# Values products regrouped from five bursts a pair to three, with their outputs copied out one unit later (attention and gated FFN, one core)

## The chip, the cores and the metric

The kernel runs on one core of one Trainium2 chip. The metric is the device time of one execution in microseconds (us), as the median of several runs. TensorE (PE) multiplies and transposes, VectorE (DVE), ScalarE (ACT) and GpSimd (POOL) work on elements, SyncE (SP) issues transfers.

## The reference, cut to what matters

```python
# q, k, v: (4, 8, 576, 64); the bias comes from a small network over the distance of two positions
scores = q @ k.transpose(0, 1, 3, 2) / 8 + bias[None]
attn = softmax(scores, axis=-1)
x = (attn @ v)                                  # the values products, (4, 8, 576, 64)
x = x.transpose(0, 2, 1, 3).reshape(4, 576, 512)
h = relu(x @ w_in)                              # 512 -> 1024
conv = depthwise_conv3(h, conv_w)               # along the sequence
out = (h * sigmoid(conv)) @ w_out               # (4, 576, 512), float32
```

## The kernel before, in words

The span has three parts. In the first 66 us the position bias is computed, written to memory, and the first attention work starts. Until about 285 us the attention runs. After that comes the feed-forward part. The change touches only the attention.

The attention goes through 16 pairs: a pair `n` is two heads of one batch. A pair has five units `t` = 0 to 4 (also called by `ui`, the same number): unit 0 holds the 64 left-over rows of both heads, units 1 to 4 hold 128 rows of each head. The list `flat` gives the units in order, and in the loop's turn for unit u each engine gets, in this order:

- PE: the scores of unit u+2 (`scores`, L349; one score tile for each head, a single one when u+2 is a unit 0). A score tile takes two PSUM banks, and the pool `psS` holds two such tiles. So the first scores of a unit can start only when the first reduction of the unit before has read its tile, and the second scores when the second reduction, and the small copy behind it, have read theirs. Then the `side` transposes (L408; none in unit 0, and L412 for the sums in unit 2), which write into the second score tile; then the transposes of unit u's probabilities (`transposes`, L420, into two of the three `psT` banks); then some parts of the values products (`pv_parts`, L457).
- DVE: the reductions of the scores of unit u+2 (`reduce`, L360: bias added, result to SBUF, row minimum kept), then the copies of unit u's transposed probabilities into `ptx` or `pty` (L91), a step of a weight-splitting job (L97 or L103), and in unit 0 the inversion of the sums (L472, L473).
- ACT: the exponentials of unit u+1 (`expo`, L374), the other copy of unit u's transposed probabilities (L88), a job step (L99), and, where a values group has ended, its copy from PSUM to `x` (L88, `act(xb...)`).

The values products of a pair come in two groups: group 0 (320 columns, from `ptx`) is complete after unit 2, group 1 (256 columns, from `pty`) after unit 4 of the pair. Each group has five parts, a part being two products (one for each head). The parts wait in the deque `fill`, and `pv_share[ui]` says how many are issued at the end of a unit. The single bank of `psO` holds a group's sum, so one group must be copied out before the next begins. In the trace each product shows as two matmul records: one part is four records, a 128-row unit's scores are eight.

Of the kernel before, what the change touches and what calls it, by code (L numbers as in the profile page):

```python
# [9 lines left out]
F32 = mybir.dt.float32  # L10
# [9 lines left out]
def attention_ffn_kernel(  # L20
# [12 lines left out]
    B, S, DM = out.shape  # L33
    NP = qk.shape[1]
# [4 lines left out]
    P = 128  # L39
# [30 lines left out]
    x_p = pool(ctx, "x", B)  # L70
# [16 lines left out]
    def act(o, i):  # L87
        nc.scalar.activation(o, i, AF.Copy)  # L88
# [45 lines left out]
    with tc.manual_schedule():  # L134
# [56 lines left out]
        x0 = x_p.tile([P, NP, S], F32, name="x0", tag="x")  # L191
# [77 lines left out]
        def bias_out(blk):  # L269
            nf, nr = reach(blk)  # L270
            n = max(nf, nr + 1)
            ps = bias_ps.pop(blk)
            st = sts[blk // 2 % 5].rearrange("p (b n) -> p b n", b=2)
            if n > 512:
                o, i = st[:, blk % 2:blk % 2 + 1], ps.rearrange("p (b a) x -> p b (a x)", b=1)
            else:
                o, i = st, ps
            fwd = nf > nr


            if n > 512 or blk % 2:
                k = relu_from(blk) - 3
                for oo, ii in (
                    (slice(nr, nr + nf), slice(0, nf)) if fwd else (slice(0, nr + 1), slice(nr, None, -1)),
                    (slice(0, nr), slice(nr, 0, -1)) if fwd else (slice(nr + 1, nr + nf), slice(1, nf)),
                ):
                    nc.scalar.activation(o[:, :, oo], i[:, :, ii], AF.Identity, bias=kv[:, k:k + 1], scale=inv_scale)  # L287
            if blk % 2 == 0:
                return
            at = 64 + (blk - 1) * P * BW - nr  # L290
            dst = bias_d[at:at + 2 * P * BW].rearrange("(b p c) -> p b c", b=2, c=BW)
            nc.sync.dma_start(dst[:, :, 0:nr + nf], st[:, :, 0:nr + nf])
# [33 lines left out]
        def turned_sp(n, t):  # L326
            tile = sp_p.tile([P, 2 * S + 2], F32R, name="sr", tag=spt[n, t][1])
            nc.scalar.activation(tile[:, 2 * S:], pars[:, 0:2], AF.Copy)
            spt[n, t] = (tile, None)
# [107 lines left out]

        ops_t = {}
        waiting = {}

        def pv_parts(n, g):
            p, b = seq[n]

            waiting[n] = waiting.get(n, 0) + 1
            x0, width = (XW, YW) if g else (0, XW)

            def part(c):
                pt, vt = ptt[n, g], vts[n]
                if c == 0:
                    ops_t[n, g] = psO.tile([P, 512], F32, name="o")  # L450
                po = ops_t[n, g]
                for h in range(2):
                    if c == 4:
                        slot, blk = (9 if h else 4), 4
                    else:
                        slot = blk = 5 + c if h else c
                    nc.tensor.matmul(  # L457
                        po[D * h:D * h + D, 0:width], vt[:, slot, :], pt[:, blk, :],
                        start=(c == 0), stop=(c == 4),
                    )  # L460
                if c == 4:
                    del ptt[n, g]
                    waiting[n] -= 1
                    if b not in xb:
                        xb[b] = x_p.tile([P, NP, S], F32, name=f"x{b}", tag="x")
                    act(xb[b][:, p, x0:x0 + width], po[:, 0:width])

            return [lambda c=c: part(c) for c in range(5)]

        def invert(n):  # L470
            sm, r = sms.pop(n), rr_t[n % 2][:, 0:9]
            nc.vector.tensor_scalar(r, sm, 1e-9, None, op0=ALU.add)  # L472
            nc.vector.reciprocal(r, r)  # L473
# [120 lines left out]
        for i in range(NBLK):  # L594
            nxt = bias_hidden(i + 1) if i + 1 < NBLK else None
            bias_mm(i, hidden)
            if last:
                bias_out(*last)
            last = (i,)
            hidden = nxt  # L600
            if i % 8 == 6 % 8 and i >= 6:
                load_bias(0, (i - 6) // 8)
            if i == 1:
                load_v(0)
            if i == 16:
                load(1)
            if i == 20:
                load_v(1)
            if i % 8 == 13 % 8 and i >= 13:
                unit = unit_steps(*first[(i - 13) // 8])  # L610
            if unit:
                next(unit, None)
            if fill:
                fill.popleft()()
        bias_out(*last)
        load_bias(0, 4)
        while fill:
            fill.popleft()()
        for _ in unit:
            pass  # L620
        for u in range(2):
            for h in heads(flat[u][1]):
                reduce(scores(*flat[u], h), *flat[u], h)
            if u == 0:
                for h in heads(flat[0][1]):
                    expo(*flat[0], h)
                turned_sp(*flat[0])
        pv_share = (2, 2, 1, 3, 2)
        hs_ff = {}
        raw_w = {}  # L630
        job_steps = iter(())
# [3 lines left out]
        for u, (n, t) in enumerate(flat):  # L635
            p, b = seq[n]
            ui = units.index(t)
            sums = n - 1 if ui == 2 and n else None
            side = None
            if u + 2 < NU:  # L640
                for h in heads(flat[u + 2][1]):
                    if side is not None:
                        reduce(side, *flat[u + 2], 0)
                    side = scores(*flat[u + 2], h)
            if t:
                if side is None:
                    side = psS.tile([P, 2, 512], F32, name="s")
                side_transposes(side, n, t, sums)
            if u + 2 < NU:
                reduce(side, *flat[u + 2], h)  # L650
            if u + 1 < NU:
                for h in heads(flat[u + 1][1]):
                    expo(*flat[u + 1], h)
                turned_sp(*flat[u + 1])
            transposes(n, t, side, sums)
            next(job_steps, None)

            parts = len(fill) if u < 5 else pv_share[ui]
            while fill and parts > 0:
                fill.popleft()()  # L660
                parts -= 1
            next(job_steps, None)
            del spt[n, t]
            if u + 2 >= NU:
                f = u + 2 - NU
                hs_ff[0, f] = ffn_in(0, f)
            if u == 1 or n and ui == 2 and n + 2 < NSEQ:
                load(2 if u == 1 else n + 2)
            if u in conv_weights:
                conv_weights[u]()  # L670

            for at, do in ((u - 7, "load"), (u - 11, "split")):
                job = at // 2
                if at % 2 == 0 or not 0 <= job < 4 * KC + 2 * FE:
                    continue
                if job < 4 * KC:
                    src, dst = w_in[job // 4 * P:job // 4 * P + P], wi[job // 4]
                else:
                    src, dst = w_out[(job - 4 * KC) // 2 * P:(job - 4 * KC) // 2 * P + P], wo[(job - 4 * KC) // 2]
                cs = slice(job % 4 * 256, job % 4 * 256 + 256) if job < 4 * KC else slice(job % 2 * 256, job % 2 * 256 + 256)  # L680
                if do == "load":
                    raw_w[job] = (e_p if job % 3 else woe_p).tile([P, 256, 2], I32, name="raw_w", tag="h")
                    load_w(raw_w[job], src[:, cs])
                else:
                    job_steps = split_w_steps(e_p, dst[:, :, cs], raw_w.pop(job), ("cv", "cv"))
            if u + 2 < NU:
                n2, t2 = flat[u + 2]
                p2, b2 = seq[n2]
                if b2 == B - 1 and p2 + 1 < NP:
                    load_bias(p2 + 1, t2)  # L690
            if ui == (0 if n > 1 else 1) and n > 0:
                invert(n - 1)
            if ui == (2 if n > 1 else 3) and 1 <= n and n + 1 < NSEQ:
                load_v(n + 1)
            if ui == 3 and n > 0:
                store_sums(n - 1)
            if ui == 4 and n > 0:
                spread_sums(n - 1)
            if ends_group(n, t):
                fill.extend(pv_parts(n, t > 2))  # L700

            if ui == 2 and n > 1:
                apply_norm(n - 2)
            if n == NSEQ - 2 and ui > 1:
                x_parts(0, ui - 2)
            if n == NSEQ - 1 and ui == 0:
                x_parts(0, 3)
            if n == NSEQ - 1 and ui in (1, 2):
                load_wo(FE - 1 + ui)
        while fill:  # L710
            fill.popleft()()
        invert(NSEQ - 1)
        turn_sums(NSEQ - 1)
        apply_norm(NSEQ - 2)
# [200 lines left out]
```

## Time and profile before

| | us |
|---|---|
| median of 3 runs | 504.41 |
| the runs | 501.97, 504.41, 504.76 |
| the profiled execution, whole time | 501.91 |
| its span, first to last instruction | 500.1 |
| PE busy | 479.1 (96%) |
| DVE busy | 386.5 (77%) |
| ACT busy | 311.1 (62%) |
| POOL busy | 103.4 (21%) |
| PE's share of the chain that ended last | 87% |
| values products (L457) in that chain | 18% |

The span is 1.81 us shorter than the profiled execution's own time. A busy PE is read with care, since matmuls overlap and their ends are modelled; what an operation costs on PE is therefore read from the start of one group of records to the start of the next, not from the busy time of a group.

### The profile page before, as it was taken

The numbers are of one execution on the slowest core, as the hardware profiler recorded it, in microseconds if no ns is written. First come the engines' busy times: TensorE is split into PE (matmuls) and PEld (weight loads), VectorE is DVE, ScalarE is ACT, GpSimd is POOL, SyncE is SP. The second block draws the span as 40 slices with busy tenths as digits, with TensorE's granted clock in tenths as the row PEclk, the third lists the DMA queues.
The fourth block names the chain that finished last, engine by engine and source line by source line (L and its number), as shares of the span: only waits on it lengthen the run. The fifth ranks groups of instructions, "written<-read, shape, count | busy, mean of one in ns | idle before, by whom it ended". The sixth has DMA issues, their size and how long they took to land.

```text
span 500.1 us, 11125 instructions
## 1 busy us (share of the span) xinstructions
PE 479.1 (96%) x4202; PEld 352.5 (70%) x4202; DVE 386.5 (77%) x875; ACT 311.1 (62%) x747; POOL 103.4 (21%) x121
## 2 busy tenths in 40 slices
PE   5988899999999999999999999899999999999994
PEld 3333256666666666666666689779988999899884
DVE  6999957888899988889898729974994299649900
ACT  5888877878888889888887736622632154126400
POOL 1000000103232313323336215620080005200000
PEclk9999999999999999999999999999999999999999
DMA  5779556488778977788751300002000200020011
GB/s 138 268 248 333 213 176 150 109 234 225 171 167 211 250 177 177 200 221 260 189 147 56 113 16 26 1 1 85 0 1 8 92 8 1 1 85 1 2 63 42
DMA packets 32703, 60.83 MB, mean 122 GB/s; under 512 B 5490, under 2 KB 12170, under 8 KB 32650
## 3 DMA queue, kind: packets, MB, share of 16 engines
q1 hardware_dynamic: 32506, 60.04, 42.2%
q8 instruction: 33, 0.54, 0.5%
q14 instruction: 20, 0.16, 0.1%
q10 hardware_dynamic: 144, 0.08, 0.1%
HBM read 44.12 MB, written 15.98 MB: 120 GB/s over the span
## 4 chain that ended last, share of the span: by engine, by line
PE 87%; DVE 5%; ACT 5%; issue 1%; DMA 1%; DVEq 0%; ACTq 0%
PE o L457 18%; PE s L518 17%; PE s L349 16%; PE tp L766 15%; PE tp L420 9%; PE s L261 6%; PE o L766 4%; ACT st L287 2%; DVE cv L741 2%; PE s L408 1%; DVE sp L360 1%; ACT y L240 1%; DMA pars<-in_par_dram 1%; ACT sp L374 1%; DVE cv L748 1%
## 5 line engine op out<-in xcount | busy, mean ns | idle before, releaser
L360 DVE CUSTOM_DVE_ANT_0 sp<-s,bt 128x576 f32<-128x576 f32 x144 | 104.2, 754 | 32.0 <-PE s L349 14.5
L374 ACT ACTIVATE sp<-sp,nm 128x576 f32<-128x576 f32 x144 | 109.9, 767 | 1.4 <-DVE nm L360 1.4
L518 PE MATMUL s<-xs,wi 128*128 128x288 f32 x768 | 103.8, 296 | 1.7 <-ACT h L530 1.7
L518 PEld LDWEIGHTS s<-xs,wi 128*128 128x128 f32 x768 | 102.8, 189 | 3.2 <-ACT h L530 2.0
L349 PE MATMUL s<-qk 64*128 64x288 f32 (+1 forms) x640 | 93.1, 431 | 1.8 <-DVE nm L360 1.1
L349 PEld LDWEIGHTS s<-qk 64*128 64x128 f32 (+1 forms) x640 | 46.8, 175 | 44.8 <-DVE nm L360 13.0
L766 PE MATMUL tp<-wo,g 128*128 128x512 f32 x288 | 70.5, 390 | 0.0
L420 PE MATMUL tp<-identr,sr 64*128 64x64 f32 x1184 | 64.3, 247 | 0.0
L741 DVE SCALAR_TENSOR_TENSOR cv<-h,cw,cv 128x575 f32<-128x575 f32 x64 | 60.6, 946 | 2.5 <-ACT cv L736 0.6
L766 PEld LDWEIGHTS tp<-wo,g 128*128 128x128 f32 x288 | 53.7, 188 | 11.6 <-DVE g L761 0.7
L420 PEld LDWEIGHTS tp<-identr,sr 64*128 64x128 f32 x1184 | 55.5, 136 | 5.7 <-issue 0.6
L457 PE MATMUL o<-ptx,vt 128*64 128x320 f32 x320 | 50.4, 443 | 1.3 <-ACT ptx L88 0.9
L261 PE MATMUL s<-y,pars 128*32 128x512 f32 (+8 forms) x352 | 46.5, 504 | 5.0 <-ACT st L287 2.2
L530 ACT ACTIVATE h<-s 128x576 f32<-128x576 f32 x32 | 20.8, 650 | 47.7 <-PE s L518 47.7
L497 POOL TENSOR_TENSOR x<-x,rb 128x576 f32<-128x576 f32 x16 | 23.6, 1473 | 128.6 <-ACT sp L374 94.2
L244 DVE TENSOR_SCALAR y<-tl,inv,nb 128x512 f32<-128x512 f32 (+8 forms) x116 | 49.9, 506 | 0.1
L457 PE MATMUL o<-pty,vt 128*64 128x256 f32 x320 | 44.2, 393 | 0.0
L261 PEld LDWEIGHTS s<-y,pars 128*32 128x32 f32 x352 | 16.4, 113 | 32.8 <-DVE y L244 17.4
L747 ACT ACTIVATE cv<-cv 128x576 f32<-128x576 f32 x32 | 21.8, 683 | 28.4 <-DVE cv L741 28.4
L91 DVE COPY ptx<-tp 128x256 f32<-128x256 f32 (+1 forms) x64 | 32.0, 500 | 1.4 <-PE tp L420 1.2
L131 POOL TENSOR_SCALAR xs<-x 128x576 fp32r<-128x576 f32 x16 | 14.8, 924 | 81.5 <-PE s L518 81.5
L88 ACT ACTIVATE ptx<-tp 128x256 f32<-128x256 f32 (+1 forms) x64 | 26.4, 438 | 7.9 <-PE tp L420 7.3
(75 smaller groups left out, 570.6 us busy)
## 6 DMA issues: line engine op xcount, KB each, us to landing
qk<-in_qk_dram SPq DMA_DIRECT2D x32, 320.0 KB
bt<-bias_d SPq DMA_DIRECT2D x32, 288.0 KB
bias_d<-st SPq DMA_DIRECT2D x14, 607.0 KB
qk<-in_qk_dram SPq DMA_DIRECT2D x32, 144.0 KB
rb<-r_d SPq DMA_DIRECT2D x32, 144.0 KB
out_dram<-o SPq DMA_DIRECT2D x17, 256.0 KB
raw_w<-in_moe_w_in_dram SPq DMA_DIRECT2D x16, 256.0 KB
raw_w<-in_moe_w_out_dram SPq DMA_DIRECT2D x12, 256.0 KB
```

The source lines that it names most:

```text
L88: nc.scalar.activation(o, i, AF.Copy)
L91: nc.vector.tensor_copy(o, i)
L244: nc.vector.tensor_scalar(y, dist[:, 0:n], inv[:, ig:ig + 1], nb1, op0=ALU.mult, op1=ALU.max)
L261: nc.tensor.matmul(ps[32 * j:32 * j + 32, a // 512 if n > 512 else blk % 2, 0:min(n - a, 512)], w2b, ys[j][:, a:min(n, a + 512)], start=Tr ...
L349: nc.tensor.matmul(ps[po, a, 0:HS], qt[rows, qo:qo + po.stop - po.start], qt[rows, KO + hh * HS:KO + hh * HS + HS], start=True, stop=True,)
L360: nc.vector.tensor_tensor_reduce(out=halves(spt[n, t][0][:, h]), in0=ps[:, :, 0:HS], in1=halves(bt[:, h]), op0=ALU.add, op1=ALU.min, scale ...
L374: exps[n, t, h] = nc.scalar.activation(sp[:, h], sp[:, h], AF.Exp, bias=nm[:, h:h + 1], scale=-1.0, accum_out=sms[n][:, col:col + 1],)
L420: tr = nc.tensor.transpose(ps[a][:, TL * s:TL * s + TL].bitcast(F32R), spf[ra, j:j + P], identr[ra, ra])
L457: nc.tensor.matmul(po[D * h:D * h + D, 0:width], vt[:, slot, :], pt[:, blk, :], start=(c == 0), stop=(c == 4),)
L518: nc.tensor.matmul(ps[:, a, 0:HS], wi[c][:, pw, cs], xss[b, c][:, px, a * HS:(a + 1) * HS], start=(i == 0), stop=(i == 3 * KC - 1),)
L741: nc.vector.scalar_tensor_tensor(out=cv[:, o:o + S - 1], in0=h[:, i:i + S - 1], scalar=cw[:, f, kk:kk + 1], in1=cv[:, o:o + S - 1], op0=AL ...
L766: nc.tensor.matmul(ps, lhs(f, gi), wo[f][:, wj, cs], start=(f == 0 and i == 0), stop=(f == FC - 1 and i == 2),)
```

## The change

`pv_share` goes from (2, 2, 1, 3, 2) to (0, 5, 0, 2, 3). Group 1, which was issued in units 0, 1 and 2 of the next pair as two, two and one part, is now issued whole at the end of unit 1. Group 0, issued as three parts in unit 3 and two in unit 4, is now issued as two and three. A group's copy out of PSUM is no longer issued right behind its last part: it is put on the list `late` and issued by `outputs()` in the next unit, behind that unit's exponentials and ahead of its copies of transposed probabilities. The first five units of the list take all parts that wait, as before.

```diff
+        late = []
+
+        def outputs():
+            while late:
+                late.pop(0)()
...
                 if c == 4:
                     del ptt[n, g]
-                    waiting[n] -= 1
-                    if b not in xb:
-                        xb[b] = x_p.tile([P, NP, S], F32, name=f"x{b}", tag="x")
-                    act(xb[b][:, p, x0:x0 + width], po[:, 0:width])
+                    late.append(lambda: out_of_psum(po))
+
+            def out_of_psum(po):
+                waiting[n] -= 1
+                if b not in xb:
+                    xb[b] = x_p.tile([P, NP, S], F32, name=f"x{b}", tag="x")
+                act(xb[b][:, p, x0:x0 + width], po[:, 0:width])
...
-        pv_share = (2, 2, 1, 3, 2)
+        pv_share = (0, 5, 0, 2, 3)
...
                 turned_sp(*flat[u + 1])
+            outputs()
             transposes(n, t, side, sums)
```

`outputs()` is also called after each step of the first loop and wherever `fill` is emptied, so no copy is lost.

On PE, over the units 0, 1 and 2 of a pair, before (in these rows a product counts once; L349 scores, L408 and L412 side transposes, L420 transposes, L457 values products):

```order
L349 MATMUL s<-qk 128x288 x4
L420 MATMUL tp<-identr,sr 128x64 x10
L457 MATMUL o<-pty,vt_106 64x256 x4
L349 MATMUL s<-qk 128x288 x4
L408 MATMUL s<-identr,sr 128x64 x2
L420 MATMUL tp<-identr,sr 128x64 x16
L457 MATMUL o<-pty,vt_106 64x256 x4
L349 MATMUL s<-qk 128x288 x4
L408 MATMUL s<-identr,sr 128x64 x2
L412 MATMUL s<-ident,rr_159 128x64 x2
L420 MATMUL tp<-identr,sr 128x64 x16
L457 MATMUL o<-pty,vt_106 64x256 x2
```

The same three units on PE, after (L462 is the values products' line there):

```order
L349 MATMUL s<-qk 128x288 x4
L420 MATMUL tp<-identr,sr 128x64 x10
L349 MATMUL s<-qk 128x288 x4
L408 MATMUL s<-identr,sr 128x64 x2
L420 MATMUL tp<-identr,sr 128x64 x16
L462 MATMUL o<-pty,vt_106 64x256 x10
L349 MATMUL s<-qk 128x288 x4
L408 MATMUL s<-identr,sr 128x64 x2
L412 MATMUL s<-ident,rr_159 128x64 x2
L420 MATMUL tp<-identr,sr 128x64 x16
```

The products of units 0 and 2 have moved into unit 1, so that in unit 0 the next unit's scores follow the transposes at once.

On ACT, where group 1 of a pair is copied to `x` (L374 exponentials, L328 a small marker copy, L88 copies), before, units 2 and 3:

```order
L374 ACTIVATE sp,sm<-sp,nm 128x576 x2
L328 ACTIVATE sr<-pars 128x2
L88 ACTIVATE ptx<-tp 128x8x64
L88 ACTIVATE x_121<-o 128x256
L374 ACTIVATE sp,sm<-sp,nm 128x576 x2
L328 ACTIVATE sr<-pars 128x2
L88 ACTIVATE pty<-tp 128x8x64
```

The same copy on ACT, after, units 2 and 3:

```order
L374 ACTIVATE sp,sm<-sp,nm 128x576 x2
L328 ACTIVATE sr<-pars 128x2
L88 ACTIVATE x_121<-o 128x256
L88 ACTIVATE ptx<-tp 128x8x64
L374 ACTIVATE sp,sm<-sp,nm 128x576 x2
L328 ACTIVATE sr<-pars 128x2
L88 ACTIVATE pty<-tp 128x8x64
```

The copy now belongs to products of the unit before and stands ahead of unit 2's copy of probabilities; nothing else on ACT has moved.

## Rows read from the trace of the kernel before

**Rows 1.** Stretches: length, busy time of each engine (instructions), PE clock, DMA share, GB/s.

```profile
60.00:80.00 20.00, 17.54 (x193) 10.20 (x191) 14.14 (x39) 16.03 (x42) 0.00 (x0) 1.00 0.49 141
82.49:281.00 198.51, 197.94 (x2273) 130.81 (x2273) 172.19 (x485) 165.04 (x460) 60.41 (x78) 1.00 0.72 186
```

**Rows 2.** Waits: waiter <- releaser: us in total, times, longest us.

```profile
ACT x L88 <- PE o L457: 14.4, 18, 1.8
```

**Rows 3.** Timeline, PE, one pair: start us, length us, what (products twice).

```profile
203.19 1.24 PE L349 MATMUL s<-qk 64*128 64x288 f32 x8
204.04 0.73 PE L420 MATMUL tp<-identr,sr 64*128 64x64 f32 x10
204.70 1.08 PE L457 MATMUL o<-pty,vt 128*64 128x256 f32 x8
205.72 1.24 PE L349 MATMUL s<-qk 64*128 64x288 f32 x8
206.58 0.41 PE L408 MATMUL s<-identr,sr 64*128 64x64 f32 x2
206.82 0.81 PE L420 MATMUL tp<-identr,sr 64*128 64x64 f32 x16
207.56 1.08 PE L457 MATMUL o<-pty,vt 128*64 128x256 f32 x8
208.57 1.24 PE L349 MATMUL s<-qk 64*128 64x288 f32 x8
...
210.49 0.65 PE L457 MATMUL o<-pty,vt 128*64 128x256 f32 x4
211.07 0.72 PE L349 MATMUL s<-qk 64*64 64x288 f32 x8
...
217.40 1.24 PE L349 MATMUL s<-qk 64*128 64x288 f32 x8
```

**Rows 4.** Timeline, PE, the first five units: ten products together, units without products.

```profile
73.98 0.76 PE L349 MATMUL s<-qk 64*128 64x288 f32 x4 [0.50 <-DVE nm L360]
...
74.60 0.82 PE L420 MATMUL tp<-identr,sr 64*128 64x64 f32 x16
75.36 0.76 PE L349 MATMUL s<-qk 64*128 64x288 f32 x4
76.33 0.72 PE L349 MATMUL s<-qk 64*128 64x288 f32 x3 [0.22 <-DVE ptx L91]
76.68 0.40 PE L408 MATMUL s<-identr,sr 64*128 64x64 f32 x1
...
80.19 2.38 PE L457 MATMUL o<-pty,vt 128*64 128x256 f32 x20
82.49 0.71 PE L349 MATMUL s<-qk 64*64 64x288 f32 x8
```

**Rows 5.** Timeline, DVE: a reduction of the first five units; reductions of later pairs.

```profile
73.16 0.76 DVE L360 CUSTOM_DVE_ANT_0 sp<-s,bt 128x576 f32<-128x576 f32 x1 [0.49 <-DMA bt<-bias_d]
...
203.99 0.76 DVE L360 CUSTOM_DVE_ANT_0 sp<-s,bt 128x576 f32<-128x576 f32 x1 [0.39 <-PE s L349]
204.67 0.08 DVE L360 DVE_READ_ACCUMULATOR2_ANT nm<- 128x1 f32 x1
204.67 0.75 DVE L360 CUSTOM_DVE_ANT_0 sp<-s,bt 128x576 f32<-128x576 f32 x1
205.35 0.08 DVE L360 DVE_READ_ACCUMULATOR2_ANT nm<- 128x1 f32 x1
205.35 0.66 DVE L91 COPY ptx<-tp 128x256 f32<-128x256 f32 x2
...
206.70 0.76 DVE L360 CUSTOM_DVE_ANT_0 sp<-s,bt 128x576 f32<-128x576 f32 x1
...
218.32 0.76 DVE L360 CUSTOM_DVE_ANT_0 sp<-s,bt 128x576 f32<-128x576 f32 x1 [0.74 <-ACT wu L99]
```

**Rows 6.** Timeline, POOL and DVE: a job step on DVE beside a POOL product.

```profile
141.85 1.53 POOL L497 TENSOR_TENSOR x<-x,rb 128x576 f32<-128x576 f32 x1
...
142.00 1.53 DVE L97 TENSOR_SCALAR wu<-raw_w 128x256 int32<-128x256 int32 x1
...
206.04 0.29 DVE L97 TENSOR_SCALAR wu<-raw_w 128x256 int32<-128x256 int32 x1
```

More of the change, by code (lines that the diff above doesn't have):

```diff
@@ L618, in attention_ffn_kernel @@
             fill.popleft()()
+        outputs()
         for _ in unit:
@@ L654, in attention_ffn_kernel @@
                 turned_sp(*flat[u + 1])
+            outputs()
             transposes(n, t, side, sums)
@@ L711, in attention_ffn_kernel @@
             fill.popleft()()
+        outputs()
         invert(NSEQ - 1)
```

## The prediction

> **What bounds the kernel now.** I read the stretches first, then the waits, then the timeline of one pair. From 82.49 to 281.00 us, which is all but the first and last of the attention's pairs, PE is busy 197.94 of 198.51 us at full granted clock, while DVE has 172.19 and ACT 165.04 us of work [rows 1]. So a pair lasts as long as PE's work in it, 14.21 us from one unit 0's scores (203.19) to the next (217.40) [rows 3], and DVE has about 13% of slack. The waits say what the delayed copy is about: ACT stands 14.4 us in 18 waits in front of a copy to `x` until the products are done [rows 2]. But ACT is not what ends a pair, PE has next to no idle time to give back (0.57 us in 198.51), and so this wait costs nothing now. I therefore look for what the change does to PE: what a burst of products costs there, and whether PE still finds its inputs ready when the bursts are placed otherwise.
>
> **The change, part by part.** I count from start to start on PE. A time within a unit is counted from the start of its first scores.
>
> *Fewer bursts.* In a pair, group 1 takes 1.02 us in unit 0 (204.70 to 205.72), 1.01 in unit 1 (207.56 to 208.57) and 0.58 in unit 2 (210.49 to 211.07), 2.61 us in all [rows 3]. The same twenty records in one burst stand in the trace, because the first five units empty the deque: 80.19 to 82.49, 2.30 us [rows 4]. The three lengths fit 0.15 us a burst and 0.1075 us a record (0.15 + 4 x 0.1075 = 0.58, + 8 x 0.1075 = 1.01, + 20 x 0.1075 = 2.30). Two bursts fewer save 2.61 - 2.30 = 0.31 us a pair. Where no burst follows, the transposes hand over to scores instead of products: 0.76 us (74.60 to 75.36) [rows 4] against 0.74 (206.82 to 207.56) [rows 3], a loss of 0.02. This leaves 0.29. It applies where group 1 of pairs 1 to 14 is multiplied, fourteen times: 14 x 0.29 = 4.1 us saved, if PE never waits. Group 0 keeps two bursts, of three and two parts before, of two and three after: nothing.
>
> *Unit 0 without products.* This is where I expect the saving to go. PE's work in unit 0 shrinks to scores and transposes: 0.85 us to the transposes (203.19 to 204.04) and 0.66 behind them (204.04 to 204.70) [rows 3], so at 1.51 us PE wants to start unit 1's scores. These need the two score tiles that unit 0's scores have just filled. The first reduction starts 0.80 us into the unit (203.99), the second 0.68 later (204.67) [rows 5]. Where scores waited for a reduction they started 0.82 us after its start (73.16 [rows 5], 73.98 [rows 4]). So unit 1's first scores start at 0.80 + 0.82 = 1.62 and its second scores at 1.48 + 0.82 = 2.30. Behind second scores that had waited, the side transposes came 0.35 us later (76.33 to 76.68) [rows 4], here at 2.65. Unhindered they would come 0.86 us behind the first scores (205.72 to 206.58) [rows 3], at 1.51 + 0.86 = 2.37. PE loses 2.65 - 2.37 = 0.28 us. Before, the burst of 1.02 us stood in this place and hid the reductions. In twelve pairs whose rows hold both starts, six first reductions came 0.80 to 0.81 after the scores and six 0.90 to 0.92 (217.40 [rows 3] to 218.32 [rows 5] is one of these); with 0.92 the loss is 0.40. I take the middle, 0.34, and keep both ends. Below nothing the loss cannot be, since the two reductions read exactly these tiles.
>
> The Trainium skill, Perfetto Trace Analysis, section Identifying Performance Opportunities, says that a gap that repeats on the engine that should be full can mean that PSUM has no room for the next tile. No row of before shows such a gap in the steady pairs; by that rule the gap stays until the score pool has another tile.
>
> *Does DVE stay late?* In unit 0 DVE's work runs from 203.99 to 206.70, 2.71 us [rows 5]; from 0.80 on, it ends at 3.51, and unit 1's reductions, whose scores are there by about 2.4, start 1.1 us late. PE does not see this: unit 1 now carries the whole burst. Its transposes follow the side transposes by 0.24, the burst follows by 0.74 (206.58, 206.82, 207.56 [rows 3]) and lasts 2.30, so unit 2 starts at 2.65 + 0.24 + 0.74 + 2.30 = 5.93. Unit 1's two reductions and copies, at 206.70 and up to about 2.4 us long by the same rows, end near 5.9 and unit 2's first reduction is due at 5.93 + 0.80 = 6.73. DVE has caught up with 0.8 us to spare.
>
> *Unit 2 without products.* PE needs 0.86 + 0.24 + 0.06 (the sums' transposes) + 0.76 = 1.92 us to unit 3's scores, and these need only the first reduction of unit 2, at 0.80 + 0.82 = 1.62. No loss. That the products of unit 3 find the last copies to `ptx` done is close, within about 0.1 us by the same lengths; I price it at nothing and keep it for the range.
>
> *The delayed copy.* Two instructions move past two exponentials and a marker copy on ACT. The exponentials no longer wait behind a copy that waits for PE. Queued behind the moved copy is the copy of transposed probabilities, which waits for transposes of its own unit anyway. The next user of `psO`, a unit after the copy, comes later than it: unit 1's burst starts 3.63 us into the pair, the copy is issued in unit 0. Gain and loss on PE: nothing; if ACT did not have the time, the cost would show as transposes that wait for exponentials. SP's load of the next values waits for group 1's products, which now end a unit earlier, and the load is issued where it was: nothing. POOL's product of `x` and the sums takes a pair that is two behind: nothing.
>
> *Sum.* Per pair -0.29 + 0.34 = +0.05 us, fourteen times: +0.7 us. From the profiled execution, 501.91 us (a span of 500.1 and 1.81 around it), this gives 502.6. That execution stands at the low end of the runs, the median of which is 504.41; so for the median I say 504.41 + 0.7 = 505.1. With the two ends of the loss, 0.28 and 0.40, it is -0.1 and +1.5 us, and with the spread of the runs (501.97 to 504.76) the forecast's own range is 503 to 507.
>
> **The rivals.**
>
> *The whole gain arrives.* If the reductions release the score tiles sooner than my lengths say, or the second scores cost nothing when they wait, the saving of 4.1 us stays: 500.3 us. For it: PE is the bound, and the saving per burst is measured. Against it: every length of the loop in unit 0 is a row, and they add to more than PE has left there.
>
> *DVE runs out of slack in unit 2.* This one ends slower. A job step on DVE that begins beside POOL's product takes 1.53 us in place of 0.29 [rows 6], 1.24 more; of the 28 such steps on the quarter-weights five are stretched to 1.30 to 1.53, all at the end of a unit 3, where DVE waits for scores anyway. If the new spacing puts the stretched step into unit 2, the first reduction of unit 3 comes 1.24 late less the slack of 0.6 that is left behind unit 2, and unit 4's second scores, which need its tile, some 0.6 us late. Five pairs of this cost 3.0 us, which gives 505.1 + 3.0 = 508.1. It decides the sign from about three pairs on. For it: DVE has no burst to hide behind in units 0 and 2. Against it: the five stretched steps lie in unit 3 now, and behind it comes a burst of three parts.
>
> *The change does nothing.* The order on PE shows that the bursts are merged, so this means only that the 0.15 us a burst moves into the neighbouring scores: 504.4, and with the loss in unit 0 up to 509. I count half of this as no change.
>
> *The clock falls.* PE will stand still for a moment in every pair. In the first units PE was busy 17.54 of 20 us and the granted clock was 1.00, the full 2.4 GHz [rows 1], with more idle time than I forecast; one pair at 1.2 GHz would add up to 14.2 us, 519 us.
> The Trainium skill, TensorE: Matmul & The Clock Gate, section A second HAM failure mode, tells of a kernel whose short stops between groups of matmuls, as it went round its PSUM banks, made the clock swing. By that rule the time would be above 510; the row above speaks against it here.
>
> **How the numbers follow.** The forecast, the gain eaten in unit 0, has 0.58. The whole gain has 0.16, DVE's slack 0.19, no effect 0.05, the clock 0.02. A measurement of this kernel can tell about 0.5%, 2.5 us, from no change, so faster means below 501.9 and slower above 506.9. Faster: the whole gain, 0.16. Slower: DVE's slack, the clock, and the upper edge of the forecast and of no effect, 0.23. The rest, 0.61, is no change. The range reaches to both neighbours, 500.3 and 508.1, with half a microsecond of the runs' spread above and none below: 500.4 to 508.6. What it leaves out is the lower half of the whole gain, the clock, and more than five stretched pairs, together under 0.2.
>
> **What would show it right or wrong.** In the timeline of PE, right: twenty products records from start to start 2.30 us in unit 1; a wait of unit 1's scores for DVE's L360 in every pair, some 0.1 us ahead of the first scores and more ahead of the second; the side transposes 2.65 us into the pair; the pair at 14.2 to 14.3 us. ACT's wait for `o` gone from the list of waits, with nothing gained by it. Wrong: a pair of 13.9 us (the whole gain), or idle time of PE in units 2 to 4 (DVE's slack), or a granted clock below 1.00 between 82 and 281 us.

## The result and the profile after

The changed kernel takes 505.1 us (median of 15 runs, 504.23 to 508.45); the kernel before, in the same comparison, 502.69 us (15 runs). The ratio is 1.0051, with an interval from 1.0029 to 1.0073: about 2.4 us, or half a per cent, slower. The profiled execution of the changed kernel took 505.47 us with a span of 503.7, that is 3.6 us more than the span of before. The stretches, with the columns of [rows 1]:

```profile
60.00:80.00 20.00, 17.41 (x192) 10.04 (x188) 13.81 (x37) 15.83 (x41) 0.00 (x0) 1.00 0.48 141
82.49:281.00 198.51, 196.31 (x2262) 131.29 (x2260) 170.62 (x482) 162.88 (x456) 60.31 (x78) 1.00 0.71 183
```

PE, which had 0.57 us of idle time in the second stretch, now has 2.20; its granted clock is 1.00 as before. One ordinary pair on PE (start, length, what; the units in the order 3 of the pair before, 0, 1, 2, 3, 4), to be set beside [rows 3]:

```profile
204.69 1.24 PE L349 MATMUL s<-qk 64*128 64x288 f32 x8
205.55 0.72 PE L420 MATMUL tp<-identr,sr 64*128 64x64 f32 x10
206.32 1.43 PE L349 MATMUL s<-qk 64*128 64x288 f32 x8
207.37 0.41 PE L408 MATMUL s<-identr,sr 64*128 64x64 f32 x2
207.62 0.83 PE L420 MATMUL tp<-identr,sr 64*128 64x64 f32 x16
208.38 2.38 PE L462 MATMUL o<-pty,vt 128*64 128x256 f32 x20
210.68 1.24 PE L349 MATMUL s<-qk 64*128 64x288 f32 x8
211.54 0.41 PE L408 MATMUL s<-identr,sr 64*128 64x64 f32 x2
211.79 0.25 PE L412 MATMUL s<-ident,rr 64*128 64x64 f32 x2
211.85 0.82 PE L420 MATMUL tp<-identr,sr 64*128 64x64 f32 x16
212.60 0.71 PE L349 MATMUL s<-qk 64*64 64x288 f32 x8
```

The five bursts have become three, and the burst of twenty records takes 210.68 - 208.38 = 2.30 us. The place to look at is 206.32: these scores are recorded as 1.43 us long and not 1.24, and the side transposes come 1.05 us behind their start and not 0.86. There is no idle time in brackets, and still PE waits, in two places. The first scores start 0.77 us behind the start of the ten transposes, where a kernel below that has no wait shows 0.56. And the second scores stand inside the group until DVE has read the second score tile. In every second pair the first of these waits is 0.1 us longer, and some of these pairs show a part of it in brackets:

```profile
190.32 1.24 PE L349 MATMUL s<-qk 64*128 64x288 f32 x8
191.18 0.72 PE L420 MATMUL tp<-identr,sr 64*128 64x64 f32 x10
192.06 1.43 PE L349 MATMUL s<-qk 64*128 64x288 f32 x8 [0.15 <-DVE nm L360]
193.11 0.41 PE L408 MATMUL s<-identr,sr 64*128 64x64 f32 x2
```

The reductions behind it, on DVE (the first row belongs to the slower pair, the second and third to the pair above):

```profile
191.23 0.76 DVE L360 CUSTOM_DVE_ANT_0 sp<-s,bt 128x576 f32<-128x576 f32 x1 [1.28 <-ACT sp L374]
...
205.50 0.76 DVE L360 CUSTOM_DVE_ANT_0 sp<-s,bt 128x576 f32<-128x576 f32 x1
...
206.18 0.76 DVE L360 CUSTOM_DVE_ANT_0 sp<-s,bt 128x576 f32<-128x576 f32 x1
```

They start 0.81 or 0.91 us behind unit 0's scores, and the next scores 0.82 or 0.83 behind each start (205.50 to 206.32, 191.23 to 192.06). From the start of one unit 3 to the next, an ordinary pair took 14.21 to 14.24 us before; now it takes 14.24 to 14.27 and 14.34 to 14.38 (one 14.42), from the fifth pair of the stretch on in turn. ACT's wait of [rows 2] is summed over the whole execution; 11.2 us of it, in 15 waits, lie between 82.49 and 281 us. For this stretch it has gone from the list of waits, and stands now at another row, the copy of transposed probabilities (into `ptx` and `pty` together 20.6 us before, 32.5 after). The second row below concerns the bias and comes up again:

```profile
ACT ptx L88 <- PE tp L420: 22.6, 27, 1.5
...
DVE sp L360 <- DMA bt<-bias_d: 1.2, 2, 0.9
```

The 3.6 us of the two profiled executions divide so. Thirteen pairs, from 82.49 to 267.99 before and from 82.81 to 269.84 after, take 1.53 more: eleven of them by 0.09 each on average, and two long ones (14.86 and 14.67, where before had one, of 14.75) the rest. The start of the stretch is 0.32 later. From the last unit 3 to the feed-forward block that follows the attention's last products it is 30.23 us (269.84 to 300.07) and not 28.87 (267.99 to 296.86), 1.36 more. The last 0.39 lies in the feed-forward part, which the change does not touch.

At that end stand waits which before did not have, the longest 1.07 us. PE and ACT:

```profile
285.18 0.83 PE L420 MATMUL tp<-identr,sr 64*128 64x64 f32 x15 [0.52 <-ACT ptx L88]
...
293.17 3.44 PE L526 MATMUL s<-xs,wi 128*128 128x288 f32 x24
297.68 2.38 PE L462 MATMUL o<-pty,vt 128*64 128x256 f32 x20 [1.07 <-ACT x L88]
```

```profile
296.65 0.65 ACT L538 ACTIVATE h<-s 128x576 f32<-128x576 f32 x1 [4.55 <-PE s L526]
297.19 0.43 ACT L88 ACTIVATE x<-o 128x320 f32<-128x320 f32 x1
```

Behind the last unit the program lays feed-forward work between the two groups. The copy of group 0, a step later now, is queued on ACT behind a relu that waits 4.55 us for that work, and PE's last burst needs the bank that the copy empties. The wait of 0.52 us at 285.18, for a late copy of probabilities, is new too; it stays in the next run (0.52 at 287.09).

### The profile page after: what moved, and what is told of

Same layout as the page of the kernel before. It is cut to its first block, busy times and chain, and to the rows that moved or that the text cites. A ratio compares the mean times of both kernels' runs of the same rounds, so it can differ in the third digit from the quotient of the medians.

```text
span 503.7 us, 11075 instructions
## 1 busy us (share of the span) xinstructions
PE 478.6 (95%) x4202; PEld 353.6 (70%) x4202; DVE 385.9 (77%) x875; ACT 310.8 (62%) x747; POOL 103.3 (21%) x121
## 4 chain that ended last, share of the span: by engine, by line
PE 77%; DVE 8%; ACT 6%; DMA 5%; issue 2%; SPq 1%; POOL 0%; DVEq 0%; ACTq 0%
PE s L526 17%; PE tp L778 15%; PE o L462 14%; PE s L349 13%; PE tp L420 7%; PE s L261 6%; PE o L778 4%; DMA bt<-bias_d 4%; DVE sp L360 2%; ACT st L287 2%; DVE cv L753 2%; ACT sp L374 1%; ACT y L240 1%; DVE ptx L91 1%; DMA pars<-in_par_dram 1%
## 5 line engine op out<-in xcount | busy, mean ns | idle before, releaser
L374 ACT ACTIVATE sp<-sp,nm 128x576 f32<-128x576 f32 x144 | 109.8, 766 | 1.6 <-DVE nm L360 1.0
L349 PE MATMUL s<-qk 64*128 64x288 f32 (+1 forms) x640 | 95.5, 435 | 3.5 <-DVE nm L360 1.7
L349 PEld LDWEIGHTS s<-qk 64*128 64x128 f32 (+1 forms) x640 | 45.8, 174 | 41.6 <-DVE nm L360 11.7
L420 PE MATMUL tp<-identr,sr 64*128 64x64 f32 x1184 | 64.6, 247 | 0.5 <-ACT ptx L88 0.5
L420 PEld LDWEIGHTS tp<-identr,sr 64*128 64x128 f32 x1184 | 55.8, 136 | 6.4 <-ACT ptx L88 0.6
L462 PE MATMUL o<-ptx,vt 128*64 128x320 f32 x320 | 50.4, 443 | 1.5 <-ACT ptx L88 0.9
L88 ACT ACTIVATE ptx<-tp 128x256 f32<-128x256 f32 (+1 forms) x64 | 26.7, 444 | 28.1 <-PE tp L420 27.7
L462 PE MATMUL o<-pty,vt 128*64 128x256 f32 x320 | 38.1, 384 | 1.1 <-ACT x L88 1.1
```

What stands on the lines that cost most here:

```text
L349: nc.tensor.matmul(ps[po, a, 0:HS], qt[rows, qo:qo + po.stop - po.start], qt[rows, KO + hh * HS:KO + hh * HS + HS], start=True, stop=True,)
L374: exps[n, t, h] = nc.scalar.activation(sp[:, h], sp[:, h], AF.Exp, bias=nm[:, h:h + 1], scale=-1.0, accum_out=sms[n][:, col:col + 1],)
L420: tr = nc.tensor.transpose(ps[a][:, TL * s:TL * s + TL].bitcast(F32R), spf[ra, j:j + P], identr[ra, ra])
L462: nc.tensor.matmul(po[D * h:D * h + D, 0:width], vt[:, slot, :], pt[:, blk, :], start=(c == 0), stop=(c == 4),)
```

## The experiments

Times are medians, each against the kernel before in the same comparison (502.26 to 502.69 us); pairs are lengths from unit 3 to unit 3.

**The end's copy at once.** The changed kernel, with the last unit's copy issued right behind its products.

```diff
             while fill and parts > 0:
...
+            if u == NU - 1:
+                outputs()
```

> The changed kernel, with one call more: in the last unit of the last pair the output of group 0 is copied out at once, ahead of the feed-forward's first relu on ScalarE. Theory (the end is a cost of its own): TensorE's wait of 1.07 us ahead of the last twenty product records goes, the steady pairs stay at 14.25 to 14.36 us, and the time is about 1 us below the changed kernel's. Rival (the wait only moves to the next step): the wait shows up behind the last products and the time stays.

504.5 us, ratio 1.0045 (1.0018 to 1.0073). The steady pairs stay at 14.24 to 14.44 us. The burst follows the feed-forward block without a wait:

```profile
295.07 3.44 PE L526 MATMUL s<-xs,wi 128*128 128x288 f32 x24
298.45 2.38 PE L462 MATMUL o<-pty,vt 128*64 128x256 f32 x20
```

The end is 29.09 us long (271.75 to 300.84) in place of 30.23. The trace shows the 1.1 us; the times, 504.5 and 505.1, lie in its direction but their intervals overlap. Two pairs of this execution are long, 14.81 and 16.51 us. In the second the granted clock fell: PE had stood 0.49 us (until 126.44) and 0.36 us (until 128.47) in a pair whose bias rows were late, and from 128.47 to 130.73 the clock was 0.53, near the lower level of 1.2 GHz. The row of this pair, with the columns of [rows 1]:

```profile
126.44:142.95 16.51, 16.00 (x165) 10.28 (x165) 12.37 (x37) 11.85 (x34) 3.66 (x5) 0.90 0.64 161
```

The kernels below with halved reductions, with (2, 3, 0, 2, 3) and with the delayed copy alone contain this edit.

**Only half of the reductions in unit 0's place.** What if DVE released the score tiles sooner? From pair 3 on, unit 2's scores are reduced and exponentiated over half of their columns, and the transposes read that half; the diff shows the reductions.

```diff
+            cut = 1 if t == 2 and n > 2 else 2
...
-                out=halves(spt[n, t][0][:, h]),
-                in0=ps[:, :, 0:HS],
-                in1=halves(bt[:, h]),
+                out=halves(spt[n, t][0][:, h])[:, 0:cut],
+                in0=ps[:, 0:cut, 0:HS],
+                in1=halves(bt[:, h])[:, 0:cut],
```

> The changed kernel with the end's copy at once, and from pair 3 on the reductions and exponentials of unit 2's scores run over half of the columns (the other half is left out, the transposes read the half that is there). These are the two reductions that VectorE makes in unit 0. Theory (unit 1's scores wait for exactly these reductions): they are shorter by some 0.3 us each, no score waits, the side transposes of unit 1 come 2.4 us into the pair, and a pair takes 13.9 to 14.0 us: some 4 us below the run with the end's copy alone. Rival (the loss in unit 0 and 1 comes from something else on TensorE, such as the hand-over from transposes to scores): side transposes at 2.65 to 2.8 and pairs of 14.25 to 14.36.

The expected 4 us do not show in the ratio (0.9998, 0.9958 to 1.0037). The eight runs behind it fall apart by their mean granted clock: 499.48 to 501.5 us at 0.994 or 0.995, 504.0 to 506.56 at 0.988 to 0.991. The kernel with the end's copy alone took 503.17 to 504.57 in its runs at 0.995 and more, so at a like clock some 3 to 4 us separate the two. That is a hint only, since the runs are sorted after the fact. The pairs are plainer: nine of thirteen take 13.83 to 13.89 us (the first lies ahead of the edit, three are long, 14.06 to 14.29). PE in unit 0 and the start of unit 1, then DVE:

```profile
201.19 1.24 PE L349 MATMUL s<-qk 64*128 64x288 f32 x8
202.05 0.72 PE L425 MATMUL tp<-identr,sr 64*128 64x64 f32 x10
202.61 1.24 PE L349 MATMUL s<-qk 64*128 64x288 f32 x8
203.47 0.41 PE L411 MATMUL s<-identr,sr 64*128 64x64 f32 x2
```

```profile
202.00 0.46 DVE L361 CUSTOM_DVE_ANT_0 sp<-s,bt 128x288 f32<-128x288 f32 x1 [0.94 <-PE s L349]
```

The first reduction starts at 0.81 as ever, is shorter, and the wait is gone: unit 1 starts at 1.42, the side transposes come at 2.28 (2.68 and 2.79 with the wait). The rival is out: the hand-over to scores costs 0.56 us, less than the 0.66 to products. So the loop from scores over the reduction to the next scores is what the change pays, and without it the merged bursts give 14.23 - 13.85 = 0.38 us a pair.

**Two parts left in unit 0.** Four bursts a pair; the delayed copy stays.

```diff
-        pv_share = (0, 5, 0, 2, 3)
+        pv_share = (2, 3, 0, 2, 3)
```

> Shares (2, 3, 0, 2, 3): group 1 in two bursts, so that unit 0 has two parts to cover its reductions; copies a unit later, the end's copy at once. Theory (a burst costs 0.15 us, and unit 0 without a burst costs 0.28 to 0.40): one burst of the five is saved and no score waits in unit 1: a pair of 14.08 us, 14 x 0.15 = 2 us below the kernel before, and unit 0 at 2.53. Rival 1 (merging bursts saves nothing): a pair of 14.23. Rival 2 (the copy to x that is now issued in unit 0 makes the first part wait for the bank): unit 0 at 2.7 or more and a pair above 14.23.

502.41 us, ratio 0.9985 (0.9952 to 1.0017), and ordinary pairs of 14.09 to 14.11. The burst fills the place where PE waited, and no group is stretched:

```profile
203.52 1.24 PE L349 MATMUL s<-qk 64*128 64x288 f32 x8
204.38 0.72 PE L420 MATMUL tp<-identr,sr 64*128 64x64 f32 x10
205.04 1.08 PE L462 MATMUL o<-pty,vt 128*64 128x256 f32 x8
206.05 1.24 PE L349 MATMUL s<-qk 64*128 64x288 f32 x8
206.91 0.41 PE L408 MATMUL s<-identr,sr 64*128 64x64 f32 x2
```

0.13 us a pair over fourteen pairs would be 1.8 us; but four pairs of this execution are long, 14.25 to 15.11. They have more than one cause. Ahead of the pair of 14.51 a reduction waits 0.73 us for bias rows. Near the end of the pair of 15.11 a reduction waits 1.83 us at the place where bias rows are late in the other kernels, though the trace names PE for it. In the pair of 14.47 a job step on DVE (L97, at 212.51) takes 1.32 us, and the scores behind it are stretched to 1.57.

**The new bursts without the delayed copy.**

```diff
-                    late.append(lambda: out_of_psum(po))
+                    out_of_psum(po)
```

> The new shares alone, each output copied at once as before. Theory (the delayed copy is needed for the merged burst): ScalarE waits for the end of the twenty records in unit 1 and for the twelve in unit 4, the exponentials stand behind it, and unit 3's products or transposes wait on TensorE: a pair of 14.4 to 14.7 us, 1 to 5 us above the changed kernel. Rival (the delayed copy is worth nothing, as the prediction had it): pairs of 14.25 to 14.36 us as in the changed kernel.

507.64 us, ratio 1.0092 (1.0056 to 1.0128): slower than the whole change. Pairs take 14.54 to 14.56 and 14.69 to 14.73 in turn. Waits from 82.49 to 281 us, then a copy on ACT, and PE's wait for a late copy of probabilities in the unit 3 before it:

```profile
ACT x L88 <- PE o L462: 31.4, 28, 1.8
...
PE tp L420 <- ACT ptx L88: 1.4, 6, 0.2
```

```profile
206.24 0.44 ACT L88 ACTIVATE x<-o 128x320 f32<-128x320 f32 x1 [1.22 <-PE o L462]
206.57 0.77 ACT L374 ACTIVATE sp<-sp,nm 128x576 f32<-128x576 f32 x1
```

```profile
200.49 0.83 PE L420 MATMUL tp<-identr,sr 64*128 64x64 f32 x15 [0.23 <-ACT ptx L88]
```

ACT stands before a copy in 28 places of the stretch (15 before), with the exponentials queued behind it, and its copies of probabilities come late for PE. With the longer bursts, ACT no longer has the time to wait; the delayed copy saves about 0.3 us a pair there.

**The delayed copy without the new bursts.**

```diff
-        pv_share = (0, 5, 0, 2, 3)
+        pv_share = (2, 2, 1, 3, 2)
```

> The delayed copies alone: shares (2, 2, 1, 3, 2) as before, each output copied out a unit later, the end's copy at once. Theory (the one bank for outputs must be empty before the next group, so a delayed copy needs a unit without products between two groups): group 0 starts in unit 3, and group 1's copy now stands behind unit 3's exponentials on ScalarE, so unit 3's products wait on TensorE some 0.5 to 1.0 us in every pair: unit 3 at 3.8 to 4.3 us, a pair at 14.8 to 15.3, the time 8 to 15 us above the kernel before. Rival (the delay costs and gives nothing by itself, as the prediction had it): a pair of 14.23.

517.29 us, ratio 1.0293 (1.0269 to 1.0318). The profiled execution of this run had a granted clock of 0.56 (746.69 us), so the rows below are those of a second one of the same kernel, at 0.989:

> The delayed copies alone once more, for an undisturbed profile. Theory: unit 3 at 3.8 to 4.3 us and a pair of 14.8 to 15.3 us, TensorE waiting in unit 3 for ScalarE's copy to x. Rival: the time of 517 us comes from another unit.

519.01 us in this single execution, with pairs of 15.00 and 15.66 in turn. Unit 3 on PE, the copy on ACT:

```profile
205.14 0.83 PE L420 MATMUL tp<-identr,sr 64*128 64x64 f32 x16
206.60 1.83 PE L462 MATMUL o<-ptx,vt 128*64 128x320 f32 x12 [0.63 <-ACT x L88]
```

```profile
206.18 0.36 ACT L88 ACTIVATE x<-o 128x256 f32<-128x256 f32 x1
```

`psO` has one bank. Before, group 1 ends in unit 2 and group 0 begins in unit 3; a copy that waits for unit 3's exponentials holds the bank until 206.54, and PE stands for 0.63 us there in this pair (in those of 15.66 for 0.96, and for 0.34 in unit 0, both for the copy). The empty unit 2 of the change is what gives the copy its time. By the lengths of the pairs each half alone is slower than both together.

**The bias loaded once.** Most long pairs begin where the bias of the next heads is due. Three kernels without the three later loads: before, the change, and (2, 3, 0, 2, 3).

```diff
-                    load_bias(p2 + 1, t2)
+                    biast[p2 + 1, t2] = biast[p2, t2]
```

> The kernel before, with the bias rows of the first two heads kept for all (the three later reloads are left out). Theory (a few pairs run long because bias rows land late): the single long pair of 14.75 us goes, all pairs are 14.21 to 14.25, and the time is about 0.5 us below the kernel before. Rival (the long pairs come from something else): a long pair near 182 us stays.

> The changed kernel with the three bias reloads left out in the same way. Theory: the long pairs of 14.86 and 14.67 us go, all pairs are 14.24 to 14.40, some 0.9 us below the changed kernel; the difference to the kernel before with one bias is then 13 x 0.09 + 1.4 at the end = 2.6 us. Rival (the bias waits do not differ between the two): the difference stays where it is with reloads and the long pairs stay.

> Shares (2, 3, 0, 2, 3) with the end's copy at once, and the three bias reloads left out. Theory (the saved burst is real, and late bias rows gave it back): no pair above 14.15 us, and the time 13 to 14 x 0.14 = about 1.9 us below the kernel before with one bias. Rival (the saving does not reach the end for another reason): the two are equal within 0.5 us although the pairs are shorter.

Measured: 501.57 us, ratio 0.9993 (0.9982 to 1.0004); 503.22 us, 1.0002 (0.9974 to 1.0031); 499.55 us, 0.9946 (0.9928 to 0.9965). The second has no long pair left, all take 14.23 to 14.26 or 14.32 to 14.37, and all of the third's take 14.09 to 14.11. The first has lost the pair of 14.75 near 182 us, but not all its pairs are short, as was expected: a new one takes 14.74 (82.33 to 97.07). There a DVE step of the sums' inversion, 0.17 us long in the steady pairs, runs beside POOL's product, as in [rows 6], and takes 1.38 us; the reductions behind it are late, and so are unit 2's scores:

```profile
91.55 1.41 POOL L497 TENSOR_TENSOR x<-x,rb 128x576 f32<-128x576 f32 x1 [89.13 <-DMA rb<-r_d]
```

```profile
91.61 1.38 DVE L472 TENSOR_SCALAR rr<-sm 128x9 f32<-128x9 f32 x1
```

Without reloads the change costs 503.22 - 501.57 = 1.65 us. The two ratios lie only 0.0009 apart and have wide intervals, but the ten runs of each kernel do not overlap (501.15 to 502.66, 502.80 to 503.81). The expected 2.6 us was too large, by some 0.5 us if the other executions have that new long pair too. That 1.65 is 0.8 less than 2.4 does not by itself show what late bias costs: the 2.4 can be 1.5 to 3.7 by its interval, and 0.5 of the 0.8 can be the new long pair. The traces show that both long pairs of the changed kernel go with the reloads; they took 0.55 us more than the long pair of before and an ordinary one together (14.86 + 14.67 against 14.75 + 14.23). Without reloads (2, 3) gains 2.0 us, as expected.

**The bias ahead of the next pair's loads.** In the loop SP issues the loads of q and k for a later pair ahead of the last rows of bias. The block that loads the bias is moved ahead of them, with (2, 3, 0, 2, 3), and on the kernel before alone.

```diff
+            if u + 2 < NU:
+                n2, t2 = flat[u + 2]
+                p2, b2 = seq[n2]
+                if b2 == B - 1 and p2 + 1 < NP:
+                    load_bias(p2 + 1, t2)
...
-            if u + 2 < NU:
-                n2, t2 = flat[u + 2]
-                p2, b2 = seq[n2]
-                if b2 == B - 1 and p2 + 1 < NP:
-                    load_bias(p2 + 1, t2)
```

> Shares (2, 3, 0, 2, 3) with the end's copy at once, and in each unit the reload of bias rows issued ahead of the next pair's q and k rows (464 KB) instead of behind them. Theory (the long pairs of the two-and-three kernel come from bias rows that land late behind these loads): the long pairs shrink, the time lies 1.0 to 1.9 us below the kernel before, near 501. Rival (the transfers as a whole are too many there, whatever their order): long pairs of 14.3 to 15 us stay, the time is equal to the kernel before within its interval.

> The kernel before with the same new order of the bias reloads alone. Theory: its one long pair of 14.75 us goes, 0.3 to 0.5 us less; all else is as before. Rival (the loads of q and k now land late): a pair above 14.3 us in another unit, the time equal or above.

With (2, 3): **500.36 us**, ratio 0.9968 (0.9953 to 0.9984), faster than both kernels, by about 2.2 us (0.3%) than before. Its interval overlaps that of (2, 3) in the old order (0.9952 to 1.0017), so what the order gives by itself rests on the traces: one long pair and not four. Twelve of thirteen pairs take 14.09 to 14.11, one 14.63, and the stretch shows PE without any idle time:

```profile
82.49:281.00 198.51, 198.51 (x2304) 133.98 (x2300) 170.79 (x489) 165.17 (x462) 60.05 (x78) 1.00 0.71 185
```

In the long pair PE waits inside a group all the same: the scores at 237.84 take 1.25 us and not 0.72, since a weight load among them waits for a transfer.

```profile
238.35 0.23 PEld L349 LDWEIGHTS s<-qk 64*64 64x64 f32 x6 [0.33 <-DMA r_d<-rt]
```

Which transfer it is stays open; the q and k rows, issued at 227.42 to 229.92 and now behind the bias, would fit.

Before with the reorder alone: 501.89 us, 0.9994 (0.9981 to 1.0008), no difference that can be measured, though the pair of 14.75 is gone from its trace.

## Why the prediction was right and where it was wrong

The forecast was 505.1 us, slightly slower and within 0.5%, and its case is the one that happened: the gain of merging is eaten in unit 0. That the time agrees to the decimal is luck. The time before was 504.41 us in the runs that the prediction had, and 502.69 in the comparison, so the base was 1.7 us too high; the predicted step was +0.7 us and the measured one +2.4, 1.7 us more. This step lies at the edge of the 2.5 us that the prediction called no change.

*Unit 0's loop: right.* Side transposes were forecast at 2.65 us, or 2.77 with the later reduction; they came at 2.68 and 2.79. The pair was forecast at 14.2 to 14.3 us and took 14.24 to 14.38. Halving the reductions removed the wait, and two parts left in unit 0 hid it. Where the loss stands was forecast less well, some 0.1 us ahead of the first scores and more ahead of the second. Of the 0.40 us, 0.21 stand ahead of the first scores (0.77 and not 0.56 behind the transposes) and 0.19 inside the group (1.05 and not 0.86); in the slower pairs it is 0.32 and 0.19. The Trainium skill (Perfetto Trace Analysis, Identifying Performance Opportunities) says that a repeating gap on the engine that should be full can mean missing room in SBUF or PSUM; the trace agrees, with the wait for a score tile that returns in every pair. A third tile was not tried, and the wait went without one when the reductions were halved (2.28 us to the side transposes).

*What merging saves, and what the loop costs: both a tenth of a microsecond a pair too small.* The mis-sized term is the hand-over behind unit 0's ten transposes. The prediction took 0.66 us, the time to products; to scores it is 0.56 (202.05 to 202.61), a row that before did not have. So the gross saving was 0.38 us a pair, not 0.29, and the loss 0.40 to 0.51 (2.68 and 2.79 against 2.28), not 0.28 to 0.40. The errors cancel: +0.02 and +0.13 in turn, about 0.08 a pair on average where +0.05 was forecast, 1.1 us in fourteen pairs for the 0.7.

*DVE in unit 1, unit 2 without products: right.* Unit 2's scores start 5.99 us into the pair (204.69 to 210.68; forecast 5.93), and unit 2 takes 1.92 us to unit 3's scores (210.68 to 212.60), as worked out, without a wait. The close call on `ptx` showed only in the long pairs:

```profile
185.47 1.30 PE L462 MATMUL o<-ptx,vt 128*64 128x320 f32 x8 [0.24 <-DVE ptx L91]
```

*The delayed copy at nothing: wrong, at both ends.* The price was worked out for a steady pair. At the end of the attention the neighbours on ACT's queue are others, and the copy went behind a relu: 1.07 us of PE's wait, and 1.1 us off the end when it was issued at once. In the steady pairs it was worth more than nothing: its absence cost 2.5 us (507.64 against 505.1), although the end is then free of that wait. The reason given, that the next user of `psO` comes a unit after the copy, is borne out: where it came in the copy's own unit, the delay cost 15 us (517.29 against 502.26). The sentence that ACT's 14.4 us of waiting cost nothing was true of the old spacing only.

*Not foreseen: late bias.* In the long pair of before the reduction waited 0.54 us for rows of bias:

```profile
180.84 0.76 DVE L360 CUSTOM_DVE_ANT_0 sp<-s,bt 128x576 f32<-128x576 f32 x1 [0.54 <-DMA bt<-bias_d]
```

In the changed kernel the trace names two such waits in the stretch. One, of 0.35 us at 183.67, stands at the pair of 14.67; the other, of 0.86 at 240.27, made no pair long (14.24 and 14.38 around it). At the pair of 14.86 the reduction came 1.26 us behind its scores (123.84 to 125.10) with no wait for bias named; there the run with the end's copy names one, of 1.53 us, and without reloads the pair is short. DMA of the bias is 4% of the changed kernel's chain and not in the page's list for before. The chain in order of time has the transfers:

```profile
168.48 5.44 DMA bt<-bias_d
173.94 9.60 DMA bt<-bias_d
...
184.75 0.68 DVE ptx L91
```

By the chain the rows landed at 183.54; the reduction that uses them began at 183.67, 0.35 us later than DVE was ready. Why the change makes them later is open, and so is how much of the 2.4 they are in the other executions; in the traces it is 0.55 us.

Together: 1.1 us in the pairs, 0.6 (by the times) to 1.1 (by the trace) at the end and 0.55 by the long pairs make 2.3 to 2.8 us, against 2.4 measured.

*The rivals.* The whole gain did not come, as no pair was near 13.9 us. The clock did not fall in the profiled execution of the change: 1.00 in both stretches. The rule on short stops between groups of matmuls (the Trainium skill, TensorE: Matmul & The Clock Gate, A second HAM failure mode) did not show there, with stops of 0.40 to 0.51 us in all in each of fourteen pairs. But the run with the end's copy, which has the same steady pairs, had one pair at 0.90, behind stops of 0.49 and 0.36 us; and the mean clock of the runs reaches down to 0.986 with the change and to 0.988 before, which would fit such falls in some executions of both kernels. That the change makes them more frequent is not shown. DVE's slack held in the changed kernel; a DVE step stretched beside POOL's product did make a long pair in two other runs (14.74 in before without reloads, 14.47 with (2, 3)). In the changed kernel a stretched job step puts off unit 4's first reduction to 202.94, but unit 4's burst of three parts hides this, and unit 0's scores start at 204.69 without a wait:

```profile
201.49 1.52 DVE L97 TENSOR_SCALAR wu<-raw_w 128x256 int32<-128x256 int32 x1
202.94 0.74 DVE L360 CUSTOM_DVE_ANT_0 sp<-s,bt 128x576 f32<-128x576 f32 x1
```

## What to carry to other kernels

Before work is taken out of a stretch of the bounding engine, add up the loop that this work was hiding there (here scores, reduction, next scores: 0.81 + 0.82 us and one reduction more) and leave as much of it as the loop needs: two parts of five did, and kept 0.13 us a pair. Of an instruction that is delayed by a step, look at the first and the last turn of the loop as well as a steady one, since the queue has other neighbours there. Look also at the transfers that just arrive in time, since a new spacing can make them late, and try the load that is due first ahead in its queue: with (2, 3) one long pair was left of four.

## What was not expected of the hardware

- The hand-over on PE depends on what follows: ten transposes to scores 0.56 us, to products 0.66. A wait can stand in the trace without idle time: a group that waits inside shows a longer record (1.43 for 1.24), and a hand-over of 0.77 for 0.56 shows none either.
- A DVE step that takes 0.17 us in the steady pairs took 1.38 beside a product on POOL (91.61, before without reloads), and the late reductions behind it made a pair of 14.74.
- The first reduction starts 0.81 or 0.91 us behind unit 0's scores, in turn from pair to pair, also without bias reloads (14.25 and 14.36 in turn). What sets this turn is open.
- Bias rows took 9.60 us (173.94 to 183.54, one piece of the chain) to land in the middle of the attention, where the DMA engines are busy 0.71 of the stretch.
